# Two layers of windowed attention and FFT convolution on one core: products one block ahead of the PV sums with two logit buffers, kernel rows permuted inside layer A, and the kernel's spectrum stored once and loaded to both halves

## The chip, the cores and the metric

The kernel runs on one core of a Trainium2 chip. The core has five engines that run their own instruction streams and wait for each other on semaphores: PE (TensorE, matrix products), DVE (VectorE), ACT (ScalarE), POOL (GpSimd) and SP (SyncE, which here only issues DMAs). The metric is the device time of one execution in microseconds, as the median of several.

## The reference

Four residual layers on one sequence of 2048 positions with 512 channels: attention, convolution, attention, convolution, each on a layer norm of x.

```python
x = A_x
x = x + _A_ref(_layernorm(x, axis=-1), A_wqkv, A_wo)
x = x + _B_ref(_layernorm(x, axis=-1), B_A_re, B_A_im, ..., B_log_dt, B_Dskip)
x = x + _A_ref(_layernorm(x, axis=-1), A_wqkv, A_wo)
x = x + _B_ref(_layernorm(x, axis=-1), B_A_re, B_A_im, ..., B_log_dt, B_Dskip)
```

Layer A has 32 heads of 16 channels. A position attends to eight positions only: itself and those 2, 4, ... 14 before it.

```python
off = jnp.arange(W) * dil                     # W, dil = 8, 2
idx = pos[:, None] - off[None, :]
...
logits = jnp.einsum("bhsd,bhswd->bhsw", q, kg) * scale
logits = jnp.where(mask[None, None, :, :], logits, -1e9)
attn = _softmax(logits, axis=-1)
o = jnp.einsum("bhsw,bhswd->bhsd", attn, vg)
return (...)(o, 0, 2, 1, 3).reshape(B, S, D) @ wo
```

Layer B convolves each channel with a kernel of 2048 taps, through a Fourier transform of length 4096. The taps come from 128 complex exponentials per channel and are the same in both B layers.

```python
K = jnp.einsum("dn,dnl,dn->dl", Cc, P, dB).real
...
Kf = rfft2(K padded to 2L);  Uf = rfft2(u padded to 2L)
y = irfft2(Uf * Kf)[..., :L] + u * Dskip
```

## The kernel before, in words

The program has these stages, one behind the other: the taps K are made and written to DRAM (`kd_dram`), together with the constants of the transforms and the front of attention layer A0; core A0; layer B0; the front of A1, mixed with the end of B0; core A1; layer B1. The times of the stages stand in the table of the next section.

**Placement of work.** Code is written in Python in the order in which a tile scheduler places it; each engine then runs its own instructions in a fixed order and waits on semaphores. Tiles come from pools with a number of buffers; an instruction that writes a tile of a full pool waits until the last user of that buffer is done. So the order of the calls and the sizes of the pools set what an engine meets next. All DMAs named below are issued by SP, in one row.

**Front of A** (`front_block`): norm of four row tiles (`xn`, applied by `ln_apply` on ACT or DVE by a list of engines), transposition by PE into `xnT`, and the projection of k into `kT_ext`.

**Core of A** (`core`): the 2048 positions are 16 tiles of 128, in four blocks q of four tiles. What a block needs:
- `qproj(q)`: 16 products on PE (L201) into four tiles `pq`, which ACT copies to `qT` (L203).
- `linit(q)`: PE writes the mask into the logit tile L (pool `ps_l`).
- `prod(q, i)`, i = 0 to 7: one DVE product of q with four shifted k (`prod`, L223, 128x2048), then 16 products on PE that sum over the channels of a head into L (L226).
- `sm_a(q)`: DVE takes the maximum (mx, L233), PE subtracts it, ACT takes the exponential (ex, L238). `sm_b(q)`: DVE sums in three steps (s, s, ssum, L244 to L248), inverts (rs, L251), and multiplies (attn, L253). The two together are the softmax chain.
- `pav(q, al)` for each tile al: two DVE products of attn with shifted v (`pav`, L264, 128x2048), which PE sums into `po` (L268); ACT copies it to `o_sb` (L271).
- `out_proj(q, al)`: PE transposes into `pt`, ACT copies to `oT` (L281), PE multiplies with `wop` into `pw` (L284; the profile calls the tile pq), and DVE adds it to the residual x_sb (L72). `pt`, `pw`, the pq of qproj and those of v share the pool `ps_q`.
- `norm_u`: the norm for layer B that follows, written into `xnT`.

`v_proj(a)` makes a tile of v on PE from `wvp` (L299), ACT copies it into `v_ext` (L301), and behind each fourth tile SP issues DMAs that copy v shifted by a position (L305, L306).

The calls are in this order before: block 0's products with all 16 v_proj between them, qproj(1); then, for each block, its softmax chain with the first four products of the next block inside, and its pav with the last four products of the next block and the qproj of the one after between them. [...]

**Taps for B0.** The taps are loaded from `kd_dram` in the row order that the transform wants by 18 DMAs (`k_load`, tile `k_rl`), called ahead of core A0. Behind the core `Dskip` is added to the first row and four copies, on DVE and ACT by turns, permute it into `k_perm` (L881).

**Layer B** (`FftB`): `f1` is the first stage of the transform (L510, 8 chunks per half of the channels; result `a1s`), `f2` the second (L519, with the 4 MB table `w_sb`, 8 chunks). In B0 they run on the taps too: `k_f2` casts a chunk to `kf_sb`, and two DMAs store it, each 64 partitions (the real or the imaginary part), twice, into two copies in `kf_dram` (L528). `u_f2` loads a chunk of 128 partitions (`kf_c`, L540, three buffers), ACT copies the input's spectrum to `ub`, and DVE makes two products t (L543, L544). `i1` and `i2` transform back; i2 reads the tables G2r and G2i. The evacuations of PSUM by `evac` (L499) go to ACT and DVE by turns.

Of the kernel before, what the change touches and what calls it, by code (L numbers as in the profile page):

```python
# [11 lines left out]
ALU = mybir.AluOpType  # L12
# [6 lines left out]
P = 128  # L19
# [87 lines left out]
class LayerA:  # L107
# [66 lines left out]
    def core(self, x_sb, u):  # L174
# [5 lines left out]
        with ExitStack() as c2:  # L180
# [7 lines left out]
            ps_q = c2.enter_context(tc.tile_pool(name=f"a{l}_ps_q", bufs=4, space=PSUM))  # L188
            ps_l = c2.enter_context(tc.tile_pool(name=f"a{l}_ps_l", bufs=1, space=PSUM))
# [170 lines left out]
def build_b_consts(nc, cpool, tmp, w2_dram):  # L360
# [78 lines left out]
    C["G2r"] = cpool.tile([P, 16, P], BF16, name="G2r"); C["G2i"] = cpool.tile([P, 16, P], BF16, name="G2i")  # L439
    for h in range(4):  # L440
        tb = tmp.tile([P, 4, P], I32, name="g2_base")
        nc.gpsimd.iota(tb[:], pattern=[[1, 4], [16, P]], base=4 * h, channel_multiplier=0)
        for nm, bias in (("G2r", 2048.0), ("G2i", 4096.0)):
# [4 lines left out]
            nc.scalar.activation(C[nm][:, h * 4:(h + 1) * 4, :], gi[:], ACT.Sin, bias=s8 * 4096, scale=-s8)  # L448
# [17 lines left out]
class FftB:  # L466


    def __init__(self, tc, nc, C, w2_dram, kf_dram, lnst, x_sb, tag):
        self.tc, self.nc, self.C, self.kf_dram, self.lnst, self.x_sb = tc, nc, C, kf_dram, lnst, x_sb  # L470
        self.w2_dram = w2_dram
        self.tag = tag
        self.c_grp, self.c_mid, self.c_ps = ExitStack(), ExitStack(), ExitStack()
        self.grp = self.c_grp.enter_context(tc.tile_pool(name=f"b{tag}_grp", bufs=5))
        self.ps = self.c_ps.enter_context(tc.tile_pool(name=f"b{tag}_ps", bufs=4, space=PSUM))
        self.nev = 0
        self.S = [dict() for _ in range(NG)]

    def open_mid(self):
        tc, nc, t = self.tc, self.nc, self.tag  # L480
        w2p = self.c_mid.enter_context(tc.tile_pool(name=f"b{t}_w2", bufs=1))
# [3 lines left out]
        self.kfp = self.c_mid.enter_context(tc.tile_pool(name=f"b{t}_kf", bufs=3))  # L485
        self.wk = self.c_mid.enter_context(tc.tile_pool(name=f"b{t}_wk", bufs=3))
# [7 lines left out]
    def evac(self, dst, src, eng=None):  # L494
        nc = self.nc
        if eng is None:
            eng = "act" if self.nev % 2 == 0 else "dve"
            self.nev += 1
# [24 lines left out]
    def k_f2(self, g):  # L523
        def consume(p2, ec):
            kf = self.wk.tile([P, DQG, EC], BF16, name="kf_sb")
            self.evac(kf[:], p2[:].rearrange("p e q -> p q e"))
            for ri in range(2):
                self.nc.sync.dma_start(self.kf_dram[g, ec, :, :, ri].rearrange("u p q e -> p u q e"),  # L528
                                       kf[ri * 64:(ri + 1) * 64].unsqueeze(1).to_broadcast([64, 2, DQG, EC]))
        yield from self.f2(g, "ka", consume)  # L530

    def u_f2(self, g):
        nc = self.nc
        t1 = self.gtile("t1", [P, DQG, P])
# [29 lines left out]
    def i2(self, g, rows_done, xo=None):  # L564
# [3 lines left out]
        for t in range(NA // 4):  # L568
            p4 = self.ptile([P, 4, DQG * 4])
            for j in range(4):  # L570
                a = t * 4 + j
                nc.tensor.matmul(p4[:, j, :], lhsT=C["G2r"][:, a, :], rhs=z[:, a, :], start=True, stop=False)
                nc.tensor.matmul(p4[:, j, :], lhsT=C["G2i"][:, a, :], rhs=z[:, NA + a, :], start=False, stop=True)
# [194 lines left out]
def k_load(tc, nc, kr, kd):  # L768
# [179 lines left out]
```

## Time and profile before

| | us |
|---|---|
| median of 3 runs | 637.56 (636.64 to 638.2) |
| the profiled execution | 638.53 |
| its span (first to last instruction) | 636.8 |
| taps, constants, front of A0 | 0 to about 150 |
| core A0 | to about 298 |
| layer B0 | to about 404 |
| front of A1 | to about 441 |
| core A1 | to about 571 |
| layer B1 | to the end |

Busy in the profiled execution: PE 390.3 us (61% of the span), DVE 479.0 (75%), ACT 355.2 (56%), POOL 42.8 (7%). The granted TensorE clock is 0.83 on average.

A group in the profile is named by its line, its engine and the tiles it writes and reads (`prod<-qT,kT_ext`). "x2" means two such instructions; [6.23 <-ACT qT L203] means that the engine was idle for 6.23 us before it, until ACT had written qT. In a table of waits the columns are the engine and the line of what waited, what it waited for, and then us in total, how often, and the longest. A table of stretches gives for each window its length, the busy time of each engine with its number of instructions, the granted clock, the share of DMA time and GB/s.

### The profile page before, as it was taken

Reading aid. Unit: us, or ns where it says so; the run is one execution under the profiler, and the core shown is the slowest. Engines: PE = TensorE matmul, PEld = TensorE weight load, DVE = VectorE, ACT = ScalarE, POOL = GpSimd, SP = SyncE. Lnnn points to the kernel's source line nnn. Section 1 sums busy time; section 2 is a strip of 40 time slices with the busy share of each in tenths; the row PEclk is TensorE's granted clock in tenths of the full one; section 3 lists DMA queues with packets and bytes.
Section 4 is the critical chain, followed back from the end, with each engine's and each line's share of the span. In section 5 each row is a group of like instructions: output and inputs, shape, how many; then the busy total and the mean of one; then the engine's idle time right before and its main releaser. Section 6 shows DMA issues by size and latency. Waiting matters only on the chain.

```text
span 636.8 us, 11210 instructions
## 1 busy us (share of the span) xinstructions
PE 390.3 (61%) x4536; PEld 251.3 (39%) x4536; DVE 479.0 (75%) x825; ACT 355.2 (56%) x605; POOL 42.8 (7%) x47
## 2 busy tenths in 40 slices
PE   1002234365862995865767377399978867558675
PEld 1001032244431453423657277244444333228664
DVE  3889999985464999884555678856688979848776
ACT  3999888976640354346645362496514243348631
POOL 1001021013100001010000000410000010100000
PEclk9999767876975898888977688799969777798779
DMA  6001210201398000000977872200300000253823
GB/s 189 1 0 59 106 68 33 86 3 39 58 316 188 1 2 1 2 0 2 362 216 205 284 257 71 68 0 17 100 2 1 1 1 3 97 223 125 265 87 132
DMA packets 30070, 58.37 MB, mean 92 GB/s; under 512 B 11193, under 2 KB 17210, under 8 KB 28466
## 3 DMA queue, kind: packets, MB, share of 16 engines
q1 hardware_dynamic: 27138, 50.84, 25.9%
q0 software_dynamic: 576, 4.19, 2.1%
q10 hardware_dynamic: 2304, 2.62, 1.3%
q8 instruction: 35, 0.57, 0.4%
q14 instruction: 17, 0.14, 0.1%
HBM read 36.57 MB, written 15.34 MB: 82 GB/s over the span
## 4 chain that ended last, share of the span: by engine, by line
DVE 34%; PE 31%; ACT 14%; DMA 10%; issue 5%; POOL 3%; SPq 1%; DVEq 0%; POOLq 0%; ACTq 0%
PE po L268 8%; DMA kf_c<-kf_dram 5%; DVE prod L223 4%; PE pq L299 4%; PE pb L510 3%; DVE x_sb L72 3%; PE pq L284 3%; DVE pav L264 3%; POOL ln_rstd L94 3%; PE pq L201 2%; DVE t L543 2%; ACT ln_junk L76 2%; DVE t L544 2%; DVE cm_a L612 2%; DVE cm_b L613 1%
## 5 line engine op out<-in xcount | busy, mean ns | idle before, releaser
L223 DVE TENSOR_TENSOR prod<-qT,kT_ext 128x2048 bf16<-128x2048 bf16 x64 | 76.1, 1217 | 20.4 <-ACT qT L203 17.8
L268 PE MATMUL po<-pav,ident 128*128 128x512 bf16 x256 | 76.8, 441 | 21.2 <-DVE pav L264 21.1
L264 DVE TENSOR_TENSOR pav<-attn,v_ext 128x2048 bf16<-128x2048 bf16 x64 | 75.3, 1219 | 7.0 <-DMA v_ext<-v_ext 5.6
L271 ACT CAST o_sb<-po 128x512 bf16<-128x512 f32 x32 | 18.7, 584 | 74.2 <-PE po L268 74.2
L268 PEld LDWEIGHTS <-ident 128*128 128x128 bf16 x256 | 27.2, 109 | 59.0 <-issue 42.2
L558 PE MATMUL pb<-Wp,t 128*128 128x128 bf16 x256 | 38.7, 245 | 17.8 <-DVE t L543 16.4
L519 PE MATMUL pb<-a1s,w_sb 128*128 128x64 bf16 x768 | 35.0, 206 | 20.0 <-ACT ub L542 6.7
L226 PE MATMUL L<-ind,prod 128*128 128x8 bf16 x1024 | 33.6, 167 | 22.2 <-DVE prod L223 22.2
L148 PE MATMUL pt<-ident,xn 128*128 128x128 bf16 x128 | 13.2, 256 | 51.7 <-DVE xn L104 49.6
L94 POOL TENSOR_TENSOR ln_rstd<-ln_veps,ln_mh 128x4 f32<-128x4 f32 x16 | 21.1, 1320 | 340.5 <-DVE ln_veps L92 317.9
L499 ACT CAST a1s<-pb 128x1024 bf16<-128x1024 f32 x30 | 30.1, 1016 | 24.4 <-PE pb L510 24.0
L542 ACT CAST ub<-pb 128x1024 bf16<-128x1024 f32 x32 | 32.3, 1023 | 19.3 <-DVE t L544 17.8
L226 PEld LDWEIGHTS <-prod 128*128 128x128 bf16 x1024 | 30.9, 99 | 29.6 <-DVE prod L223 24.6
L76 ACT ACTIVATE ln_junk<-x_sb 128x512 bf16<-128x512 f32 x48 | 30.3, 632 | 18.5 <-DVE x_sb L72 16.5
L519 PEld LDWEIGHTS <-w_sb 128*128 128x128 bf16 x768 | 31.2, 106 | 23.5 <-issue 18.1
L284 PE MATMUL pq<-wop,oT 128*128 128x512 bf16 x128 | 34.0, 389 | 10.5 <-ACT oT L281 10.1
L559 PE MATMUL pb<-WpJ,t 128*128 128x128 bf16 x256 | 38.0, 246 | 0.4 <-DVE t L544 0.3
L154 PE MATMUL pp<-xnT,wqk 128*128 128x512 bf16 x128 | 32.9, 398 | 7.4 <-ACT xnT L150 4.2
L746 PE MATMUL pk<-B_r,A_r 128*128 128x84 bf16 x128 | 18.5, 267 | 28.9 <-DVE A_r L614 28.9
L558 PEld LDWEIGHTS <-t 128*128 128x128 bf16 x256 | 28.2, 111 | 17.1 <-DVE t L543 17.0
L72 DVE SCALAR_TENSOR_TENSOR x_sb<-pq,x_sb 128x512 f32<-128x512 f32 x32 | 22.0, 687 | 15.9 <-PE pq L284 15.9
L543 DVE TENSOR_TENSOR t<-ub,kf_c 128x1024 bf16<-128x1024 bf16 x32 | 22.1, 690 | 14.4 <-DMA kf_c<-kf_dram 11.9
(205 smaller groups left out, 1017.7 us busy)
## 6 DMA issues: line engine op xcount, KB each, us to landing
kf_c<-kf_dram SPq DMA_DIRECT2D x32, 512.0 KB, 4.7
w_sb<-w_dram SPq DMA_DIRECT2D x8, 1024.0 KB, 11.2
kf_dram<-kf_sb SPq DMA_DIRECT2D x32, 256.0 KB, 3.8
x_sb<-in_A_x_dram POOLq DMA_DIRECT2D x4, 1024.0 KB, 10.0
v_ext<-v_ext SPq DMA_DIRECT2D x6, 448.0 KB, 6.1
wqk<-in_A_wqkv_dram SPq DMA_DIRECT2D x4, 512.0 KB, 4.8
xin<-in_A_x_dram SPq DMA_DIRECT2D x4, 512.0 KB, 9.2
w_dram<-w_full SPq DMA_DIRECT2D x4, 512.0 KB, 2.6
```

The lines of the kernel that those rows point to most:

```text
L72: nc.vector.scalar_tensor_tensor(x_row, y_psum, 1.0, x_in, ALU.mult, ALU.add, accum_out=lnst["s1"][:, a, part:part + 1])
L76: nc.scalar.activation(lnst["junk"][:], x_row, ACT.Square, accum_out=lnst["s2"][:, a:a + 1])
L94: nc.gpsimd.tensor_tensor(rstd[:], veps[:], lnst["mh"][:, 0:n], ALU.pow)
L223: nc.vector.tensor_tensor(pr[:], qT[:, ft].unsqueeze(1).to_broadcast([P, NW, 4, P]), kap, ALU.mult)
L226: nc.tensor.matmul(L[:, al, w0 + wi, ft * 8:(ft + 1) * 8], lhsT=pr[:, wi, al, :], rhs=ind8[:], start=False, stop=True, skip_group_check=True)
L264: nc.vector.tensor_tensor(pv[:], attn[:, al, wg * NW:(wg + 1) * NW, :].unsqueeze(2).to_broadcast([P, NW, DH, H]), vap, ALU.mult)
L268: nc.tensor.matmul(po[:], lhsT=ident[:], rhs=pv[:, wi].rearrange("p d h -> p (d h)"), start=(w == 0), stop=(w == W - 1))
L284: nc.tensor.matmul(pw[:], lhsT=oT[:, ftp, :], rhs=wo[:, ftp, :], start=(ftp == 0), stop=(ftp == NDT - 1))
L519: nc.tensor.matmul(p2[:, j, :], lhsT=self.w2[:, ec * EC + j, :], rhs=a1s[:, ec * EC + j, :], start=True, stop=True)
L543: nc.vector.tensor_tensor(t1[:, :, ec * EC:(ec + 1) * EC], ub[:], kc[:, 0], ALU.mult)
L558: nc.tensor.matmul(p3[:, j, :], lhsT=t1[:, dql, :], rhs=wp_r, start=True, stop=False)
L559: nc.tensor.matmul(p3[:, j, :], lhsT=t2[:, dql, :], rhs=wpj_r, start=False, stop=True)
```

## The change

**1. Core.** Products run one more block ahead: those of blocks 0 and 1 ahead of the first pav, then two of block q+2 behind each tile's pav of block q; blocks 2 and 3 have pav alone. The softmax chain of block q+1 is split around the pav of block q. The projections of v move from block 0's products to block 1's. Two blocks' logits are alive at once, so `ps_l` has two buffers; `ps_q` has two instead of four.

```diff
-            ps_q = c2.enter_context(tc.tile_pool(name=f"a{l}_ps_q", bufs=4, space=PSUM))
-            ps_l = c2.enter_context(tc.tile_pool(name=f"a{l}_ps_l", bufs=1, space=PSUM))
+            ps_q = c2.enter_context(tc.tile_pool(name=f"a{l}_ps_q", bufs=2, space=PSUM))
+            ps_l = c2.enter_context(tc.tile_pool(name=f"a{l}_ps_l", bufs=2, space=PSUM))
...
                 prod(0, i)
-                if i % 2 == 1:
-                    for a in range(2 * (i - 1), 2 * (i + 1)):
-                        v_proj(a)
-            qproj(1)
+                if i == 3:
+                    qproj(1)
+                    linit(1)
+            sm_a(0)
+            for i in range(8):
+                v_proj(2 * i)
+                v_proj(2 * i + 1)
+                prod(1, i)
+                if i == 3:
+                    sm_b(0)
             for q in range(4):
                 n1 = q + 1 if q + 1 < 4 else None
                 n2 = q + 2 if q + 2 < 4 else None
-                sm_a(q)
                 if n1 is not None:
-                    linit(n1)
-                    prod(n1, 0)
-                    prod(n1, 1)
-                sm_b(q)
-                if n1 is not None:
-                    prod(n1, 2)
-                    prod(n1, 3)
+                    sm_a(n1)
+                if n2 is not None:
+                    qproj(n2)
+                    linit(n2)
                 for al in range(4):
                     pav(q, al)
+                    if al == 1 and n1 is not None:
+                        sm_b(n1)
                     if al > 0:
                         out_proj(q, al - 1)
-                    if al == 1 and n2 is not None:
-                        qproj(n2)
-                    if n1 is not None:
-                        prod(n1, 4 + al)
+                    if n2 is not None:
+                        prod(n2, 2 * al)
+                        prod(n2, 2 * al + 1)
                 out_proj(q, 3)
                 for qq in ((), (0, 1), (2,), (3,))[q]:
                     norm_u(qq)
+                if hook is not None:
+                    hook(q)
```

DVE in core A0, before, from the normaliser of block 0 (attn_1899) to the first pav; L_1852 and attn_2203 are of block 1:

```order
L253 TENSOR_TENSOR attn_1899<-ex_1847,rs_1897 128x1024
L223 TENSOR_TENSOR prod_2024<-qT_1821,kT_ext_101 128x2048
L223 TENSOR_TENSOR prod_2071<-qT_1821,kT_ext_101 128x2048
L223 TENSOR_TENSOR prod_2118<-qT_1821,kT_ext_101 128x2048
L233 TENSOR_REDUCE mx_2150<-L_1852 128x128
L244 TENSOR_TENSOR s4_2195<-ex_2151 128x512
L246 TENSOR_TENSOR s2_2197<-s4_2195 128x256
L248 TENSOR_TENSOR ssum_2199<-s2_2197 128x128
L251 RECIPROCAL rs_2201<-ssum_2199 128x128
L253 TENSOR_TENSOR attn_2203<-ex_2151,rs_2201 128x1024
L264 TENSOR_TENSOR pav_1938<-attn_1899,v_ext_1516 128x2048
```

The same place in the changed kernel; attn_1885 is of block 0, L_1672 and attn_2119 of block 1, qT_2017 of block 2:

```order
L253 TENSOR_TENSOR attn_1885<-ex_1748,rs_1883 128x1024
L233 TENSOR_REDUCE mx_2011<-L_1672 128x128
L223 TENSOR_TENSOR prod_2060<-qT_2017,kT_ext_102 128x2048
L244 TENSOR_TENSOR s4_2111<-ex_2012 128x512
L246 TENSOR_TENSOR s2_2113<-s4_2111 128x256
L223 TENSOR_TENSOR prod_2078<-qT_2017,kT_ext_102 128x2048
L248 TENSOR_TENSOR ssum_2115<-s2_2113 128x128
L223 TENSOR_TENSOR prod_2135<-qT_2017,kT_ext_102 128x2048
L251 RECIPROCAL rs_2117<-ssum_2115 128x128
L223 TENSOR_TENSOR prod_2153<-qT_2017,kT_ext_102 128x2048
L253 TENSOR_TENSOR attn_2119<-ex_2012,rs_2117 128x1024
L264 TENSOR_TENSOR pav_2046<-attn_1885,v_ext_1518 128x2048
```

Block 1's chain stands ahead of the first pav in both. Now four products of block 2 stand between its steps. In all, 16 products precede the first pav in core A0 before, and 20 now; in core A1, 14 and 19.

**2. Taps.** `k_load` and the permutation run inside core A0, in two halves of 256 channels, behind blocks 1 and 2, through one half-sized buffer. All four copies are on ACT.

```diff
+    def k_half(h):
+        hs = slice(h * 256, (h + 1) * 256)
+        kr = krp.tile([P, NA, D // 2], BF16, name="k_rl")
+        k_load(tc, nc, kr, kd, hs)
+        nc.vector.tensor_tensor(kr[0:1, 0, :], kr[0:1, 0, :], dsk[:, hs], ALU.add)
+        for h2 in range(2):
+            nc.scalar.copy(kp[:, h * 64 + h2 * 32:h * 64 + (h2 + 1) * 32, :, :],
+                           kr[:, :, h2 * 128:(h2 + 1) * 128].rearrange("p a (q r) -> p q a r", r=4))
+
+    la.core(x_sb, u, lambda q: k_half(q - 1) if q in (1, 2) else None)
```

SP in core A0, before, where v_ext is shifted:

```order
L787 DMA k_rl<-kd_dram 32x2x512
L787 DMA k_rl<-kd_dram 64x5x512
L787 DMA k_rl<-kd_dram 64x7x512
L787 DMA k_rl<-kd_dram 64x4x512
L172 DMA wop<-in_A_wo_dram 32x4x512 x4
L305 DMA v_ext<-v_ext 112x1024
L306 DMA v_ext<-v_ext 15x1024
```

And in the changed kernel:

```order
L780 DMA kd_dram<-kgs 1x64
L172 DMA wop<-in_A_wo_dram 32x4x512 x4
L305 DMA v_ext<-v_ext 112x1024
L306 DMA v_ext<-v_ext 15x1024
L305 DMA v_ext<-v_ext 112x2048
L306 DMA v_ext<-v_ext 15x2048
L305 DMA v_ext<-v_ext 112x2048
L306 DMA v_ext<-v_ext 15x2048
L787 DMA k_rl<-kd_dram 16x16x256
```

The loads of k_rl stood ahead of all shifts of v_ext; now they follow, but for one between the last two pairs.

**3. Spectrum.** `kf_dram` holds the spectrum once. A chunk is stored by two DMAs of half the size as before and loaded by two DMAs of 64 partitions each, one to either half of a slot of `kf_ring`, which has four slots.

```diff
-                self.nc.sync.dma_start(self.kf_dram[g, ec, :, :, ri].rearrange("u p q e -> p u q e"),
-                                       kf[ri * 64:(ri + 1) * 64].unsqueeze(1).to_broadcast([64, 2, DQG, EC]))
+                self.nc.sync.dma_start(self.kf_dram[g, ec, :, ri], kf[ri * 64:(ri + 1) * 64])
...
-            kc = self.kfp.tile([P, 2, DQG, EC], BF16, name="kf_c")
-            nc.sync.dma_start(kc[:], self.kf_dram[g, ec].rearrange("u p i q e -> (u p) i q e"))
+            kc = self.kf_ring[:, self.nkf % 4]
+            self.nkf += 1
+            for h in range(2):
+                nc.sync.dma_start(self.kf_ring[h * 64:(h + 1) * 64, (self.nkf - 1) % 4], self.kf_dram[g, ec])
```

SP from the end of core A0 through layer B0, before:

```order
L306 DMA v_ext<-v_ext 15x2048
L878 DMA dskip<-in_B_Dskip_dram 1x512
L484 DMA w_sb<-w_dram 128x4096 x4
L528 DMA kf_dram<-kf_sb 64x2x1024 x32
L540 DMA kf_c<-kf_dram 128x2048 x16
```

And in the changed kernel:

```order
L803 DMA k_rl<-kd_dram 64x4x256
L493 DMA w_sb<-w_dram 128x4096 x4
L494 DMA g_sb<-g_dram 128x4096
L541 DMA kf_dram<-kf_sb 64x1024 x32
L556 DMA kf_ring<-kf_dram 64x2048 x32
```

The stores keep their number at half the elements, the loads double in number at half the size, and all loads of B0 still follow all its stores.

**4. Smaller parts.** The tables G2r and G2i are no longer resident: while the constants are made, they are written to `g2_dram` by eight DMAs, through one buffer `g2_s`, and each layer B loads them (`g2_sb`, 1 MB, L494). In the front of A1 three of four norm applications go to DVE instead of two: `["act", "dve", "act", "dve"]` became `["act", "dve", "dve", "dve"]`. Four pools of layer B got the option by which a buffer's waits are kept for each tile apart (`reuse_waits="tile"`).

More of the change, by code (lines that the diff above doesn't have):

```diff
@@ L496, in evac @@
         if eng is None:
-            eng = "act" if self.nev % 2 == 0 else "dve"
+            eng = self.pat[self.nev % len(self.pat)]
             self.nev += 1
@@ L866 @@
     krctx = ExitStack()
-    krp = krctx.enter_context(tc.tile_pool(name="kr", bufs=1, side="right"))
-    kr = krp.tile([P, NA, D], BF16, name="k_rl")
-    k_load(tc, nc, kr, kd)
-    la.core(x_sb, u)
-    z0 = xnT[:].rearrange("p t c -> p (t c)").rearrange("p (m c) -> p m c", m=2 * NA)
-    fb = FftB(tc, nc, C, w2_dram, kf_dram, lnst, x_sb, 0)
-    fb.z0 = z0
-    kp = fb.gtile("k_perm", [P, P, NA, 4])
-    with tc.tile_pool(name="dsk", bufs=1) as dp:
-        dsk = dp.tile([1, D], BF16, name="dskip")
-        nc.sync.dma_start(dsk[:], ins["Dskip"].partition_broadcast(1))
-        nc.vector.tensor_tensor(kr[0:1, 0, :], kr[0:1, 0, :], dsk[:], ALU.add)
-    for h in range(4):
-        (nc.vector.tensor_copy if h % 2 == 0 else nc.scalar.copy)(
-            kp[:, h * 32:(h + 1) * 32, :, :], kr[:, :, h * 128:(h + 1) * 128].rearrange("p a (q r) -> p q a r", r=4))
-    krctx.close()
-    la.close()
+    kpp = krctx.enter_context(tc.tile_pool(name="kp", bufs=1))
+    kp = kpp.tile([P, P, NA, 4], BF16, name="k_perm", tag="kp")
+    krctx2 = ExitStack()
+    krp = krctx2.enter_context(tc.tile_pool(name="kr", bufs=1, side="right"))
+    dsk = krp.tile([1, D], BF16, name="dskip")
+    nc.sync.dma_start(dsk[:], ins["Dskip"].partition_broadcast(1))
+    def k_half(h):
[7 more added lines that the diff above has]
+    la.core(x_sb, u, lambda q: k_half(q - 1) if q in (1, 2) else None)
+    krctx2.close()
+    la.close()
+    z0 = xnT[:].rearrange("p t c -> p (t c)").rearrange("p (m c) -> p m c", m=2 * NA)
+    fb = FftB(tc, nc, C, w2_dram, g2_dram, kf_dram, lnst, x_sb, 0)
+    fb.z0, fb.ring_pool = z0, kpp
     fb.open_mid()
```

54 lines of the change are left out of this document (33 added, 21 removed).

## The prediction

> **What bounds the kernel now.** I read the table of stretches first, cut at the stages, to see which engine fills which stage (columns: window, length, busy time of PE, PEld, DVE, ACT, POOL, granted TensorE clock, DMA share, GB/s).
>
> ```profile
> 178.00:206.00 28.00, 11.49 (x154) 6.17 (x152) 15.66 (x20) 6.27 (x9) 0.00 (x0) 0.61 1.10 246
> 206.00:260.00 54.00, 44.15 (x414) 22.42 (x414) 51.34 (x72) 22.68 (x46) 2.04 (x2) 0.85 0.01 1
> 260.00:298.00 38.00, 24.64 (x137) 10.62 (x135) 27.19 (x50) 17.86 (x37) 2.92 (x2) 0.94 0.00 0
> ...
> 318.00:348.00 30.00, 20.26 (x427) 18.37 (x426) 16.05 (x14) 14.04 (x15) 0.00 (x0) 0.73 0.73 211
> 348.00:386.00 38.00, 20.62 (x379) 18.94 (x375) 26.75 (x38) 18.30 (x19) 0.36 (x1) 0.77 0.72 239
> 404.00:441.00 37.00, 27.94 (x164) 13.80 (x162) 22.80 (x58) 28.32 (x52) 10.04 (x5) 0.86 0.13 30
> ...
> 467.00:520.00 53.00, 44.05 (x344) 21.10 (x344) 44.72 (x60) 20.91 (x41) 1.01 (x1) 0.80 0.00 1
> 520.00:571.00 51.00, 33.21 (x260) 15.42 (x258) 39.48 (x70) 19.47 (x42) 3.92 (x3) 0.82 0.22 84
> ```
>
> Both attention cores are DVE's: 51.34 of 54 us, then 27.19 of 38 in the first; 44.72 of 53 and 39.48 of 51 in the second. The exception is 178 to 206, where DVE works 15.66 of 28 us while DMA is full. From 318 to 348, storing the kernel's spectrum, no engine is full (PE 20.26 of 30) and DMA is 0.73 busy.
>
> Next I read what DVE waited for, by stage: the first core, the first layer B, the second core (columns: us in total, times, longest).
>
> ```profile
> DVE prod L223 <- ACT qT L203: 14.3, 4, 6.2
> DVE x_sb L72 <- PE pq L284: 6.0, 5, 1.8
> DVE pav L264 <- DMA v_ext<-v_ext: 5.6, 1, 5.6
> DVE mx L233 <- PE L L226: 4.8, 3, 3.4
> DVE s L244 <- ACT ex L238: 4.7, 3, 2.2
> ```
>
> ```profile
> DVE kf_sb L499 <- DMA kf_dram<-kf_sb: 11.0, 7, 5.4
> DVE a1s L499 <- PE pb L510: 10.0, 8, 2.8
> DVE t L543 <- DMA kf_c<-kf_dram: 8.9, 9, 3.2
> ```
>
> ```profile
> DVE x_sb L72 <- PE pq L284: 9.9, 9, 1.8
> ...
> DVE s L244 <- ACT ex L238: 3.2, 3, 1.3
> DVE mx L233 <- PE L L226: 3.1, 3, 1.3
> ```
>
> So there are three targets: the head of core A0, where pav waits for the shifted copies of v; the softmax chain (mx, Exp on ACT, s), met when DVE has nothing else ready; and the spectrum stores, on which 11.0 us of kf_sb casts wait.
>
> **Term 1, head of core A0.** The timeline of SP, then of DVE:
>
> ```profile
> 184.50 4.94 SPq L787 DMA_DIRECT2D k_rl<-kd_dram  x5
> ...
> 192.64 0.59 SPq L305 DMA_DIRECT2D v_ext<-v_ext  x1
> ```
>
> ```profile
> 156.43 2.36 DVE L223 TENSOR_TENSOR prod<-qT,kT_ext 128x2048 bf16<-128x2048 bf16 x2 [6.23 <-ACT qT L203]
> 162.34 1.23 DVE L223 TENSOR_TENSOR prod<-qT,kT_ext 128x2048 bf16<-128x2048 bf16 x1 [3.54 <-ACT qT L203]
> ```
>
> ```profile
> 205.90 1.22 DVE L264 TENSOR_TENSOR pav<-attn,v_ext 128x2048 bf16<-128x2048 bf16 x1 [5.59 <-DMA v_ext<-v_ext]
> ```
>
> SP issues the last loads of k_rl from 184.50 on, and only at 192.64 the first v_ext shift; the first pav starts at 205.90. The change takes k_rl out of that place, so the shifts follow the projections of v, and DVE's own work sets the first pav. A prod costs 2.36/2 = 1.18 us. What one softmax chain costs DVE, and where it stands, the second core's head shows:
>
> ```profile
> 453.09 1.23 DVE L233 TENSOR_REDUCE mx<-L 128x128 bf16<-128x1024 f32 x1 [1.33 <-PE L L226]
> 457.83 3.50 DVE L223 TENSOR_TENSOR prod<-qT,kT_ext 128x2048 bf16<-128x2048 bf16 x3 [3.52 <-ACT qT L203]
> 461.35 0.43 DVE L244 TENSOR_TENSOR s<-ex 128x512 bf16<-128x512 bf16 x1
> ...
> 462.48 1.23 DVE L223 TENSOR_TENSOR prod<-qT,kT_ext 128x2048 bf16<-128x2048 bf16 x1
> 463.62 0.95 DVE L251 RECIPROCAL rs<-ssum 128x128 bf16<-128x128 f32 x1
> ...
> 465.56 0.68 DVE L253 TENSOR_TENSOR attn<-ex,rs 128x1024 bf16<-128x1024 bf16 x1
> ...
> 467.29 1.22 DVE L264 TENSOR_TENSOR pav<-attn,v_ext 128x2048 bf16<-128x2048 bf16 x1
> ```
>
> The three sums run from 461.35 to the prod at 462.48, 1.13 us; with mx, rs and attn a chain is 1.23 + 1.13 + 0.95 + 0.68 = 3.99 us. In DVE's order of before, 16 prods and two chains precede the first pav; now it is 20 prods and two chains. Two prods run before 162.34, so 18 x 1.18 + 2 x 3.99 = 29.2 us follow. I add the longest wait of each kind that the stage shows, 3.4 (mx) and 2.2 (ex), and get 162.3 + 29.2 + 5.6 = 197: 8.9 us earlier, with four more prods done (4 x 1.18 = 4.7 us). Gain 13.6 us. Ends: no more than the v_ext wait of 5.6 us, where something else holds the copies; or 19 us, where the waits vanish too.
>
> **Term 2, rest of core A0.** Chains a block ahead spare what is left of the mx and ex waits: 4.8 + 4.7 less the 5.6 already used is 3.9 us; I take half, 2. Against it stands ps_q with two buffers instead of four: the pt and pw tiles of one output projection fill both, and the next waits for DVE's residual add (x_sb, L72). Ends 4 better to 6 worse, the latter the whole x_sb wait over again. The k_perm copies go to ACT in this stage: 2 x 3.70 us by the row below, on an ACT that is busy 22.68 of 54 and 17.86 of 38 us. An o_sb or oT behind such a pair is late by up to 3.7 us, twice; I cost it at nothing, since in block 1 DVE has two prods to do between the pavs of one tile and the next; for block 2, where no prods are left as cover, up to 4 us stand in the ends.
>
> **Term 3, core A0 to layer B.**
>
> ```profile
> 293.43 0.69 DVE L72 SCALAR_TENSOR_TENSOR x_sb<-pq,x_sb 128x512 f32<-128x512 f32 x1 [0.97 <-PE pq L284]
> ...
> 298.07 1.29 DVE L881 COPY k_perm<-k_rl 128x2048 bf16<-128x2048 bf16 x2 [0.55 <-ACT xnT L102]
> ```
>
> ```profile
> 298.07 3.70 ACT L881 COPY k_perm<-k_rl 128x2048 bf16<-128x2048 bf16 x2
> ```
>
> ```profile
> 298.97 5.16 PE pb L510 x96
> ```
>
> The first transform (f1, L510) now starts at 298.97, after the last norm and the first k_perm copy. With k_perm built inside the core, only PSUM must be free, which the last residual add gives: 293.43 + 0.69 = 294.1. Gain 4.8 us; the ends are 0 (its casts queue behind the norm on DVE and ACT) and 5. The w_sb loads, which wait for k_perm now, come earlier by more than f1 does, so they aren't late next; g2_sb adds one transfer behind them, used much later.
>
> **Term 4, spectrum stores.**
>
> ```profile
> 308.80 39.85 SPq L528 DMA_DIRECT2D kf_dram<-kf_sb  x32
> ```
>
> ```profile
> 320.17 1.08 PE pb L510 x16
> ...
> 324.72 1.01 PE pb L519 x16
> ```
>
> Sixteen chunks take 39.85 us, 2.49 each. Halving the bytes takes the DMA from 0.73 busy to about 0.37, and then PE is next: one group of L510 and one of L519, 1.08 + 1.01 = 2.09 us, x16 = 33.4. Gain 6.4 us. Ends: 9 with a higher granted clock than 0.73, and 3 where the casts' other wait (a1s for PE, 10.0 us) grows.
>
> **Term 5, spectrum loads.** Each chunk's load becomes two of 64 partitions, in a ring of four instead of three. Chunks run from 354.46 to 384.47:
>
> ```profile
> 354.46 0.69 DVE L543 TENSOR_TENSOR t<-ub,kf_c 128x1024 bf16<-128x1024 bf16 x1 [3.16 <-DMA kf_c<-kf_dram]
> ```
>
> ```profile
> 384.47 0.68 DVE L544 TENSOR_TENSOR t<-ub,kf_c 128x1024 bf16<-128x1024 bf16 x1
> ```
>
> That is 30.7/16 = 1.92 us each. The fourth slot can take back part of the 8.9 us of load waits; the first load still goes out behind the last store, so the 3.16 us of first fill stay. I put 0, with ends of 6 better and, by the next row, 18 worse over both layers. The nearest row for 64-partition transfers is the store stretch, 211 GB/s; at that rate a chunk's 524 KB take 2.48 us, 0.56 more than now, x32 = 18 us. I stay at 0 because there half the time nothing was to be sent (0.73 busy): 211/0.73 = 289 GB/s while busy makes 1.81 us a chunk, under the 1.92.
>
> [...]
>
> **Term 6, front and core of A1.** Four norm applications go from ACT to DVE, which has room there (22.80 of 37 us against ACT's 28.32): I put 1 us, ends 0 and 3, the latter if ACT bounds the whole stage.
>
> In the core five more prods and one mx stand ahead of the first pav: 5 x 1.18 + 1.23 = 7.1 us moved into the head, whose 3.52 us of qT wait can cover part; I put the first pav at 469.5, 2.2 later than 467.29, so 5 us gained. Of the mx and ex waits, 3.1 + 3.2, I take 3. Gain 8, ends 2 and 14. Layer B1 has no stores; 0.
>
> The eight stores of the G2 table before core A0 and the DMAs for it replace two resident tiles; ACT's next Sin waits for the previous store. I put 0, 1 either way.
>
> **Sum.** 13.6 + 2 + 4.8 + 6.4 + 0 + 1 + 8 = 35.8 us. The terms are from one execution of 638.53 us (span 636.8), 0.97 above the median of 637.56; against the median: 637.56 - 35.8 = 601.8.
>
> **Rivals.** A: forecast, 592 to 612. B: the cores stay as slow per block as now, DVE waiting elsewhere (x_sb for pq grew from 6.0 to 9.9 between the cores); then terms 2 and 6 give 0 or -4 and the gain is 13.6 + 4.8 + 6.4 - 4 = 21: 617. For it: DVE already works 51.34 of 54 us from 206 to 260, so nothing is to be had there; against it: 44.72 of 53 and 39.48 of 51 in the second core. C: half loads at the row's 211 GB/s, term 5 at -18: 620. D, the other side: two pq buffers. Each of 32 output projections waits for the residual add of the one before, which stands on DVE behind up to two prods and a pav (2 x 1.18 + 1.22 = 3.6 us). The change is undone from 35.8/32 = 1.12 us per projection on the path; at 1.5 us it takes 650. Against it: the waits of L72 today go the other way, DVE for PE. E: all waits in the cores gone, k_f2 at 1.9 us a chunk: 36 + 5 + 6 + 3 = 50, 588.
>
> **Chances.** A 0.55, B 0.17, C 0.12, D 0.05, E 0.08; 0.03 for a failure that leaves the time unchanged. The range 586 to 622 takes in A, B, most of E and C. A difference within 0.3% (2 us) can't be told from none. Faster 0.92, same 0.03, slower 0.05.
>
> **What would show it.** First pav near 197, f1 less than 1 us after the last residual add; sixteen stores' chunks in about 33 us with no kf_sb wait for DMA; u_f2 chunks at or under 1.92 us (2.5 is C); mx and s waits of DVE near zero in both cores. D would show as PE waiting for DVE x_sb ahead of L284 or the transposes. Wrong outright if the first pav waits for v_ext still, or ACT's k_perm pairs leave PE waiting for oT.

## The result, and the profile after

The changed kernel takes 603.33 us (601.58 to 605.19) against 637.1 for the kernel before on the same chip: a ratio of 0.9472, 95% interval 0.9437 to 0.9507. The forecast was 601.8, the range 586 to 622. The profiled execution has a span of 599.8 us, 37.0 less than before. The sum was right, and three of its terms were wrong by 6 to 10 us, not all in one direction. That the time came out so near is in part luck, as the account below shows. (In `e1_core_only` and `e10_prefetch` one execution of four was disturbed and slower; their times below are the medians of the other three, and in `e1_core_only` it was the profiled one, so that no durations are read from its trace.) The table of the stages shows them; every time in it is the start (or, for a "last", the end) of the row named, in the timelines of the two profiled executions.

| from row to row | before | after | gained | forecast |
|---|---|---|---|---|
| start to first pav of A0 | 205.9 | 196.7 | 9.2 | 8.9 |
| to the end of A0's last residual add | 88.2 | 79.5 | 8.7 | 6.7 |
| to the first f1 matmul | 4.9 | 0.1 | 4.8 | 4.8 |
| to the first spectrum store | 9.8 | 10.6 | -0.8 | 0 |
| to the end of the last store's issue | 39.9 | 26.9 | 13.0 | 6.4 |
| to the first product t | 5.8 | 6.4 | -0.6 | 0 |
| to the last product t of B0 | 30.7 | 36.3 | -5.6 | 0 |
| to the first ln_rstd of A1 | 19.2 | 20.6 | -1.4 | 0 |
| to the first pav of A1 | 62.9 | 66.3 | -3.4 | -1.2 |
| to the end of A1's last residual add | 100.9 | 82.8 | 18.1 | 10.1 |
| to the last product t of B1 | 44.3 | 48.7 | -4.4 | 0 |
| to the end of the span | 24.3 | 24.9 | -0.5 | 0 |

The forecast's 4.7 us for the four products stand in the second row with term 2's 2; term 6 is spread over the rows to and behind A1's first pav (front 1, first pav 2.2 later, 7.1 us of work moved ahead and 3 of waits).

The table of stretches of the changed kernel, in the columns explained above, cut at its own stages:

```profile
197.00:241.00 44.00, 36.12 (x335) 18.65 (x342) 42.80 (x58) 20.00 (x37) 0.00 (x0) 0.92 0.08 20
...
287.00:314.00 27.00, 19.85 (x549) 17.57 (x550) 18.77 (x17) 17.45 (x18) 0.00 (x0) 1.00 0.68 151
...
320.00:338.00 18.00, 5.09 (x76) 4.44 (x76) 10.35 (x16) 7.47 (x8) 0.00 (x0) 0.51 1.04 229
...
443.00:491.00 48.00, 39.18 (x377) 20.12 (x383) 47.12 (x63) 18.39 (x37) 0.00 (x0) 0.93 0.06 16
```

DVE is now busy 42.80 of 44 us behind the first pav of A0 and 47.12 of 48 in A1: hardly a wait is left in these two stretches. In the store stretch (287 to 314) TensorE is granted its full clock, where it had 0.73 on average. From 320 to 338, the loads of the spectrum, DMA is full (1.04) at only 229 GB/s, and DVE works 10.35 of 18 us.

What DVE waited for in core A0 from the first pav on, and from A1's front through core A1:

```profile
DVE x_sb L72 <- PE pq L284: 5.3, 4, 3.0
DVE pav L264 <- DMA k_rl<-kd_dram: 2.5, 1, 2.5
```

```profile
DVE ln_nb L96 <- POOL ln_rstd L94: 6.8, 7, 1.2
DVE kT_ext L157 <- PE pp L154: 6.7, 6, 2.1
DVE x_sb L72 <- PE pq L284: 5.0, 3, 2.6
DVE mx L233 <- PE L L226: 2.1, 2, 1.7
```

No wait of s for ex is left among the longer ones, mx waits 2.1 instead of 3.1 us, and x_sb's waits for pq fell from 9.9 (nine times) to 5.0 (three times). Ahead of the first pav of A0 the gain in such waits is smaller: from 150 on, mx still waits 4.7 us there (4.8 in all of core A0 before), s 0.2 (4.7), and prod for qT 8.9 (14.3). And the first pav itself still waits for DMAs:

```profile
196.72 1.23 DVE L264 TENSOR_TENSOR pav<-attn,v_ext 128x2048 bf16<-128x2048 bf16 x1 [2.49 <-DMA k_rl<-kd_dram]
```

In layer B0 the list reads:

```profile
DVE t L559 <- DMA kf_ring<-kf_dram: 10.5, 9, 2.6
DVE kf_sb L512 <- DMA kf_dram<-kf_sb: 5.1, 4, 1.7
DVE a1s L512 <- PE pb L523: 3.7, 5, 1.2
```

The kf_sb casts still wait 5.1 us for stores (11.0 before), and the products t wait longer than before for their loads (10.5 against 8.9 us). The DMA issues, from the page (KB each, median us to landing):

```profile
kf_ring<-kf_dram SPq DMA_DIRECT2D x64, 256.0 KB, 7.2
...
kf_dram<-kf_sb SPq DMA_DIRECT2D x32, 128.0 KB, 3.4
```

A load of half the size lands after 7.2 us, where 512 KB took 4.7.

### The profile page after: what moved, and what is told of

It reads as the page before. It is cut to its first block, busy times and chain, and to the rows that moved or that the text cites. A ratio compares the mean times of both kernels' runs of the same rounds, so it can differ in the third digit from the quotient of the medians.

```text
span 599.8 us, 11233 instructions
## 1 busy us (share of the span) xinstructions
PE 373.9 (62%) x4496; PEld 242.2 (40%) x4536; DVE 475.8 (79%) x828; ACT 356.8 (59%) x603; POOL 44.8 (7%) x47
## 4 chain that ended last, share of the span: by engine, by line
DVE 34%; PE 26%; DMA 12%; ACT 11%; issue 9%; SPq 3%; POOL 3%; DVEq 0%; POOLq 0%; ACTq 0%; another core or an unknown queue 0%
DMA kf_ring<-kf_dram 5%; DVE pav L264 5%; PE po L268 4%; PE pq L299 4%; DVE prod L223 3%; POOL ln_rstd L94 3%; PE pq L201 3%; PE pb L523 2%; DMA v_ext<-v_ext 2%; PE pq L284 2%; DVE cm_a L628 2%; PE L L226 2%; PE pp L154 2%; DMA kf_dram<-kf_sb 2%; DVE x_sb L72 2%
## 5 line engine op out<-in xcount | busy, mean ns | idle before, releaser
L268 PE MATMUL po<-pav,ident 128*128 128x512 bf16 x245 | 69.2, 402 | 19.7 <-DVE pav L264 18.0
L268 PEld LDWEIGHTS <-ident 128*128 128x128 bf16 x256 | 25.8, 103 | 51.1 <-issue 30.6
L76 ACT ACTIVATE ln_junk<-x_sb 128x512 bf16<-128x512 f32 x48 | 30.2, 630 | 26.9 <-DVE x_sb L72 26.7
L94 POOL TENSOR_TENSOR ln_rstd<-ln_veps,ln_mh 128x4 f32<-128x4 f32 x16 | 23.1, 1444 | 307.8 <-DVE ln_nm L87 154.7
L226 PEld LDWEIGHTS <-prod 128*128 128x128 bf16 x1024 | 32.8, 96 | 21.8 <-DVE prod L223 12.2
L532 PE MATMUL pb<-a1s,w_sb 128*128 128x64 bf16 x768 | 32.3, 199 | 12.3 <-ACT ub L558 8.2
L226 PE MATMUL L<-ind,prod 128*128 128x8 bf16 x1024 | 35.0, 167 | 6.4 <-DVE prod L223 6.2
L574 PEld LDWEIGHTS <-t 128*128 128x128 bf16 x256 | 28.4, 112 | 24.3 <-DVE t L559 24.2
L762 PE MATMUL pk<-B_r,A_r 128*128 128x84 bf16 x128 | 18.1, 263 | 30.8 <-DVE A_r L630 30.7
L532 PEld LDWEIGHTS <-w_sb 128*128 128x128 bf16 x768 | 28.4, 102 | 15.3 <-issue 11.6
L559 DVE TENSOR_TENSOR t<-ub,kf_ring 128x1024 bf16<-128x1024 bf16 x32 | 22.0, 686 | 14.6 <-DMA kf_ring<-kf_dram 14.6
L201 PE MATMUL pq<-xnT,wqk 128*128 128x512 bf16 x121 | 31.9, 386 | 2.5 <-ACT qT L203 1.3
## 6 DMA issues: line engine op xcount, KB each, us to landing
x_sb<-in_A_x_dram POOLq DMA_DIRECT2D x4, 1024.0 KB, 10.6
```

The lines of the kernel that those rows point to most:

```text
L94: nc.gpsimd.tensor_tensor(rstd[:], veps[:], lnst["mh"][:, 0:n], ALU.pow)
L201: nc.tensor.matmul(pq[:], lhsT=wqk[:, dt, ft * P:(ft + 1) * P], rhs=xnT[:, dt, q * 512:(q + 1) * 512], start=(dt == 0), stop=(dt == NDT - 1))
L226: nc.tensor.matmul(L[:, al, w0 + wi, ft * 8:(ft + 1) * 8], lhsT=pr[:, wi, al, :], rhs=ind8[:], start=False, stop=True, skip_group_check=True)
L268: nc.tensor.matmul(po[:], lhsT=ident[:], rhs=pv[:, wi].rearrange("p d h -> p (d h)"), start=(w == 0), stop=(w == W - 1))
L532: nc.tensor.matmul(p2[:, j, :], lhsT=self.w2[:, ec * EC + j, :], rhs=a1s[:, ec * EC + j, :], start=True, stop=True)
L574: nc.tensor.matmul(p3[:, j, :], lhsT=t1[:, dql, :], rhs=wp_r, start=True, stop=False)
```

## The experiments

The ratios are against the kernel before on the same chip. The first four kernels part the change.

**Core alone (`e1_core_only`).** The kernel before with the new `core` of part 1, word for word, and nothing else.

> The kernel before with the new order of the core and its PSUM split (two pq, two L), and nothing else: the 18 loads of k_rl stay ahead of core A0, the spectrum is stored twice. Theory (the head of core A0 needs both the order and the freed queue): the shifts of v_ext still go out at about 192 to 200, so the first pav stays near 205.9; what comes behind it shortens as in the changed kernel (8.7 us), core A1 gives its 14.7 us (18.1 behind its first pav less 3.4 ahead of it), the front of A1 nothing: 637 - 23 = 614 us. Rival (the order alone makes the head): 9.2 us more, 604 to 605.

Measured: 607.6 us, ratio 0.9532 (0.9482 to 0.9583), between the two. SP's rows and the first pav:

```profile
170.14 17.24 SPq L792 DMA_DIRECT2D k_rl<-kd_dram  x17
188.53 2.58 SPq L172 DMA_DIRECT2D wop<-in_A_wo_dram  x4
191.21 0.59 SPq L305 DMA_DIRECT2D v_ext<-v_ext  x1
```

```profile
208.16 1.16 DVE L264 TENSOR_TENSOR pav<-attn,v_ext 128x2048 bf16<-128x2048 bf16 x1
```

All loads of k_rl still go out ahead of the first v_ext shift, and the first pav comes at 208, not at 197: the order alone doesn't make the head. But DVE doesn't wait for v_ext there, as it did before for 5.59 us. The scheduler has placed the same calls in another order: 24 products and three chains, the last without its attn, stand ahead of that pav, where the changed kernel has 20 products and two chains. At the prediction's prices these are 4 x 1.18 + 3.31 = 8.0 us of work that is done early and is missing behind the pav, so the late pav costs less than the theory's 9.2 us. The order alone brings some 30 us (a ratio of 0.9532 on 638.1), the whole change 33.8.

**Core undone (`e4_old_core`).** The changed kernel with the `core` of before and a call of the hook added to it.

> The changed kernel with part 1 undone: the core in the order of before, with four pq and one L buffer; taps in the core, spectrum stored once, G2 loaded. Theory: core A1 goes back by 14.7 us, core A0 behind the first pav by 8.7; the head keeps part of its gain, since the shifts of v_ext need not wait for k_rl, at most the 5.6 us that pav waited before: 603 + 23 + 4 = 630 us. Rival (the k_rl loads alone held the head): first pav near 197 to 198, 626 to 627 us.

Measured: 637.2 us, ratio 0.9976 (0.9952 to 1.0001). Both expectations were too low: without the new order the rest of the change brings nothing. In its trace the head did move, and the time was given back. The first row is its first pav; the next two are what DVE waited for from there to the end of the core, with its table of stretches:

```profile
193.82 1.23 DVE L264 TENSOR_TENSOR pav<-attn,v_ext 128x2048 bf16<-128x2048 bf16 x1 [4.16 <-DMA k_rl<-kd_dram]
```

```profile
DVE x_sb L72 <- PE pq L284: 13.2, 11, 2.9
DVE pav L264 <- DMA k_rl<-kd_dram: 4.2, 1, 4.2
```

```profile
206.00:260.00 54.00, 40.89 (x377) 20.79 (x380) 44.59 (x69) 26.38 (x42) 3.87 (x2) 0.75 0.08 20
```

First pav 12.1 us earlier than before, but 103.4 us from there to the last residual add instead of 88.2. DVE waits 13.2 us for output projections, where it waited 6.0, and works 44.59 of the 54 us from 206 to 260 instead of 51.34; the granted clock there is 0.75 instead of 0.85. Before, the softmax chain of block 1 was done ahead of the wait for v_ext; here it comes behind the first pav, with one of the products. A head that starts sooner with less work done ahead is not a gain. Of the 13.2 us, the three longest waits (7.4 us) stand in the last block, from 287 on, where no copy of k_perm runs any more (the last starts at 243.94); so the copies don't explain the most of it. What the lower clock takes isn't parted from the rest by any run. Part of why nothing is left lies elsewhere: this kernel also has part 3, which loses time as it stands (below).

**Spectrum stored twice again (`e2_stored_twice`).** Part 3 undone, the ring of four slots kept:

```diff
-                self.nc.sync.dma_start(self.kf_dram[g, ec, :, ri], kf[ri * 64:(ri + 1) * 64])
+                self.nc.sync.dma_start(self.kf_dram[g, ec, :, :, ri].rearrange("u p q e -> p u q e"),
+                                       kf[ri * 64:(ri + 1) * 64].unsqueeze(1).to_broadcast([64, 2, DQG, EC]))
...
-            for h in range(2):
-                nc.sync.dma_start(self.kf_ring[h * 64:(h + 1) * 64, (self.nkf - 1) % 4], self.kf_dram[g, ec])
+            nc.sync.dma_start(kc, self.kf_dram[g, ec].rearrange("u p i q e -> (u p) i q e"))
```

> The changed kernel with part 3 undone but for the four slots: the spectrum is stored twice and a chunk is loaded by one DMA of 128 partitions. Theory (storing once gives 13 us, loading by halves of 64 partitions takes 10 us): B0's store stretch goes back from 26.9 to about 39 us, the chunks of u_f2 go from 2.27 to 1.9 us or less in both layers; sum +2 to +4, about 606 us. Rival (the loads are slow because of the ring or the waits, not the 64 partitions): loads stay at 2.2 us a chunk, about 616 us.

Measured: 590.2 us, ratio 0.9263 (0.923 to 0.9295): 13 us faster than the changed kernel, where both theories had it slower. SP's rows, and the stretch of the loads:

```profile
287.44 37.32 SPq L541 DMA_DIRECT2D kf_dram<-kf_sb  x32
324.86 25.62 SPq L556 DMA_DIRECT2D kf_ring<-kf_dram  x16
```

```profile
331.00:345.00 14.00, 6.73 (x96) 6.09 (x96) 11.48 (x18) 8.36 (x9) 0.00 (x0) 0.50 0.94 325
```

The stores go back by 10.4 us, as expected. But the products t of a layer now take 25.6 us in B0 (36.3 in the changed kernel) and 25.1 in B1 (34.6), a pace of 1.6 us a chunk: better than before (30.7 and 30.3), so the four slots may have a gain of their own that the half loads hid. The next kernel tests it.

**Three slots (`e7_ring3`).** That kernel with `[P, 3, 2, DQG, EC]` and `% 3`.

> The kernel e2_stored_twice with three slots in the ring instead of four, one DMA of 128 partitions for each chunk. Theory (before, the loads were bound by latency over three buffers, so that the fourth slot gives what the two layers gain, 1.92 to 1.6 us a chunk): 590 + 10 = 600 us, 1.9 us a chunk. Rival (the fourth slot is not what counts, but the finer waits of the pools): 590 us.

Measured: 599.9 us, ratio 0.9374 (0.9319 to 0.9429). The stretches of t are 30.5 and 31.3 us, as before the change. The fourth slot alone is worth some 10 us over both layers (61.8 us of these stretches against 50.7). But for the finer waits of the ring, this kernel is the change without its part 3: against `e1_core_only` (0.9532), parts 2 and 4 bring it to 0.9374, and part 3 takes the changed kernel back to 0.9472. In the same window DMA is no longer full:

```profile
331.00:345.00 14.00, 4.61 (x71) 4.01 (x70) 9.64 (x16) 7.08 (x7) 0.00 (x0) 0.50 0.73 240
```

With three slots the loads wait for room (0.73 busy, 240 GB/s), with four they fill the DMA (0.94, 325 GB/s).

**Halves from two copies (`e9_halves_two_copies`).** `e2_stored_twice` with its load split into halves, each from its own copy, to part two causes.

```diff
-            nc.sync.dma_start(kc, self.kf_dram[g, ec].rearrange("u p i q e -> (u p) i q e"))
+            for h in range(2):
+                nc.sync.dma_start(self.kf_ring[h * 64:(h + 1) * 64, (self.nkf - 1) % 4], self.kf_dram[g, ec, h])
```

> The kernel e2_stored_twice (590.2 us) with one edit: a chunk is loaded by two DMAs of 64 partitions, each from its own stored copy. It tells two causes of the slow loads apart, both halves reading one place in DRAM, or the 64 partitions. Theory (64 partitions): the chunks of u_f2 go to 2.2 to 2.3 us in both layers, DMA full at about 229 GB/s, 590 + 20 = 610 us. Rival (reading one place twice): 1.6 us a chunk as in e2, 590 us.

Measured: 611.3 us, ratio 0.9567 (0.9513 to 0.9622).

```profile
331.00:345.00 14.00, 4.05 (x64) 3.56 (x63) 7.77 (x12) 5.75 (x6) 0.00 (x0) 0.50 1.04 246
```

The same bytes from the same places, cut at partition 64: 246 GB/s at a DMA share of 1.04, against 325 at 0.94, and 21 us more. So it is the cut at partition 64, not the place that is read. A load is also half as large, and no run cuts it in half another way. But its packets are as large as those of the whole load (some 4 KB in both windows), and DMA is full, so the packets themselves take longer: by share and rate, 4 KB cost 1.04 x 16 x 4096 B / 246 GB/s = 0.28 us of an engine's time, against 0.94 x 16 x 4096 B / 325 GB/s = 0.19 us in the window of `e2_stored_twice`. It isn't the gaps between loads. Why the packets take longer, no run shows.

**Two queues (`e5_two_queues`).** The changed kernel with the upper halves issued by ACT (`for h, q in enumerate((nc.sync, nc.scalar)): q.dma_start(...)`).

> The changed kernel with one edit: of the two loads of a chunk, the lower half of the partitions stays on SP's queue and the upper half is issued by ACT, so that both halves are under way at once. [...] Rival (the sum of the halves is limited whatever the queue): 2.27 us a chunk, 603 us, or more by ACT's issues.

Measured: 593.8 us, ratio 0.9288 (0.9249 to 0.9328): 9.5 us faster than the changed kernel, but not by faster transfers.

```profile
320.00:335.00 15.00, 5.46 (x92) 4.71 (x88) 9.32 (x15) 6.07 (x6) 0.00 (x0) 0.62 0.99 225
```

```profile
q1 hardware_dynamic: 597, 1.92, 56.7%
q10 hardware_dynamic: 431, 1.44, 41.6%
```

Both queues are at work in that window (packets, MB, share), and together they move 225 GB/s at a share of 0.99: no more than one queue. The time came from elsewhere: with ACT's halves off SP's row, loads no longer stand behind all stores, and the first t starts at 315.96, 0.9 us ahead of the last store's issue end instead of 6.4 behind it. That is 4.2 us, of which B0's products t, in 38.3 instead of 36.3 us, give 2.0 back. The rest of the 9.6 us between the two spans is spread over the later stages, 3.3 of it behind the last t of B1, and stays unexplained.

**One load for both halves (`e3_one_load`).** The changed kernel with a single DMA that reads the chunk twice, by a leading dimension of step zero: `nc.sync.dma_start(kc, bass.AP(tensor=src.tensor, offset=src.offset, ap=[[0, 2]] + [list(x) for x in src.ap]))`.

> The changed kernel with one edit: a chunk is stored once and loaded by one DMA that reads it twice into all 128 partitions, instead of two DMAs of 64. [...] Rival (reading one place twice, or the ring, is the limit): no change, 603.

Measured: 817.6 us, ratio 1.2821 (1.2794 to 1.2847). It was expected to be faster or, by the rival, the same; both were wrong. The DMA view from 327 to 470:

```profile
DMA packets 1855, 7.51 MB, mean 53 GB/s; under 512 B 28, under 2 KB 28, under 8 KB 1852
...
q1 hardware_dynamic: 1852, 7.47, 12.8%
```

A share of 12.8% is about that of two of the sixteen engines (2/16 = 12.5%), at 53 GB/s where the half loads had 229. Why this load runs so, no run shows.

**Three pq (`e8_pq3`).** `ps_q` with three buffers, `ps_o` with one.

> The changed kernel with three pq buffers instead of two and one po instead of two. Theory (two pq buffers cost nothing, since DVE waits for the output projection only in the tails): no gain, 603; one po buffer may cost up to 0.6 us a tile, up to 620. Rival D of the prediction (projections wait for a pq slot): less than 600.

Measured: 609.5 us, ratio 0.9546 (0.9495 to 0.9598), 6 us slower than the changed kernel. Both cores are longer (86.7 and 85.8 us from the first pav to the last residual add, instead of 79.5 and 82.8; some 2.8 us of A0's difference is a product, an rs and an attn that stand ahead of the pav in the changed kernel and behind it here). In core A0 PE now waits for the copy of po, which it doesn't in the changed kernel:

```profile
PE po L268 <- ACT o_sb L271: 9.4, 6, 3.4
```

So the second po is worth more than a third pq; since this run changes both, pq alone isn't measured. Against rival D speaks the trace of the changed kernel: its list of PE's waits from either first pav to the last residual add has none for x_sb.

**The old split of the norm (`e11_old_split`).** `["act", "dve", "act", "dve"]` in the changed kernel.

> The changed kernel with one edit: the norm applications of A1's front go to ACT and DVE by turns again. Term 6 of the prediction gave the new split 1 us. Theory now (DVE stands still for 5.9 us beside the memset, so that a third application on DVE waits behind it): the stretch from the first ln_rstd of A1 to the first pav gets 1 to 2.5 us shorter, 601 to 603 us. Rival (the new split helps): 604 to 606.

Measured: 601.9 us, ratio 0.9412 (0.9361 to 0.9463). The stretch to A1's first pav is 64.0 us instead of 66.3, as the theory said, but that is no gain: 17 products stand ahead of that pav now, where the changed kernel has 19, and these two, at 1.18 us each, make the 2.3 us. From that pav to the last residual add it takes 85.8 instead of 82.8 us, so front and core together take 149.8 instead of 149.1, and the time as a whole can't be told from 603.3. Neither split is shown to be better.

**GpSimd's memset (`e6_zero_dma`, `e12_before_zero_dma`).** In the front of A1, in every kernel so far, one POOL row lies beside a row of DVE. The timelines of POOL and of DVE in the changed kernel:

```profile
378.06 6.06 POOL L308 MEMSET v_ext<- 1x7168 bf16 x1
```

```profile
378.23 5.92 DVE L85 TENSOR_SCALAR ln_nm<-ln_nm 128x4 f32<-128x4 f32 x1
```

A tensor_scalar of 128x4 that takes 0.16 us elsewhere takes 5.92, until the memset ends. By what the one holds up the other, the trace doesn't show. Both experiments replace `nc.gpsimd.memset(v[0:1, 0:14, :], 0.0)` by a DMA from a row of zeros in DRAM.

> The kernel e2_stored_twice (590.2 us) with one edit: the first row of v_ext is cleared by a DMA of zeros instead of GpSimd's memset. In the front of A1 that memset runs 6.06 us, and DVE's tensor_scalar at its side takes 5.9 us, before and after the change alike. Theory (DVE stands still because of the memset): the front shortens by 4 to 6 us, about 585 us. Rival (the front is bound by something else then): within 1 us of 590.

> The kernel before with one edit: the first row of v_ext is cleared by a DMA of zeros instead of GpSimd's memset, in both layers. Theory (DVE's tensor_scalar in the front of A1 stands still for as long as the memset runs, and the front waits for it): the stretch from the first ln_rstd of A1 to the first pav falls from 62.9 to 58 or 59 us, 633 us. Rival (in the old order the front is bound by ACT, so that DVE's stop is hidden): within 2 us of 637.6.

Measured on `e2_stored_twice`: 584.6 us, ratio 0.9137 (0.9077 to 0.9197) against 0.9263 (0.923 to 0.9295); the stretch to A1's first pav is 62.1 us instead of 66.3. On the kernel before: 628.8 us, ratio 0.9866 (0.984 to 0.9892); that stretch is 57.6 instead of 62.9. In both pairs the same number of products stands ahead of that pav (19, and 14), so the stretches can be compared. The theory holds, in both orders; on the kernel before, more is gained than these 5.3 us, most of it in core A1 (97.7 instead of 100.9 us from its first pav to its last residual add), which stays unexplained.

**Early loads (`e10_prefetch`).** `e6_zero_dma` with the first four ring loads of B0 ahead of the stores of the second half.

> The kernel e6_zero_dma (584.6 us) with one edit: the first four loads of layer B0's ring are issued ahead of the stores of the second half of the channels, instead of behind all stores. Theory (the fill of the ring, 5.8 us from the last store's end to the first product t, is exposed): 4 to 6 us off, about 580 us. Rival (they only push the stores back): 584 to 586.

Measured: 580.3 us, ratio 0.9102 (0.9024 to 0.918), not told apart from `e6_zero_dma`. The fill is gone (first t at 325.08, before the stores' end at 329.35), but the stores take 43.4 us instead of 38.6: kf_sb's waits for stores are 15.1 us in its list. Both beat the changed kernel and the one before; the least measured is 580.3 us, 9% under the kernel before.

## Why the prediction was right, and where its terms were not

- **What bounds it** held: both cores were DVE's, and what the new order removed is DVE's waits. It is most of the gain: alone it brings some 30 of the 33.8 us, and the rest of the change without it brings nothing (a ratio of 0.9976).
- **Term 1** (13.6 us): first pav at 197 forecast, 196.72 measured, with 20 products and two chains ahead of it as worked out. But "DVE's own work sets the first pav" is not what the trace shows: the pav waits 2.49 us for DMAs, and a wait for v_ext there was a sign by which the forecast would be wrong outright. In the chain of waits the third pair's shift of v_ext takes 13.15 us, and one load of k_rl, which lies between the last two pairs, ends last:

```profile
181.43 13.15 DMA v_ext<-v_ext
...
194.59 2.13 DMA k_rl<-kd_dram
```

The waits from the third product on sum up to 7.8 us instead of 5.6 (4.72 of them mx), the work is 27.7 instead of 29.2, and it starts 1.1 us sooner; that these cancel is luck. The place of k_rl has a smaller worth than the rows say, since with a late pav more work is placed ahead of it (`e1_core_only`).
- **Term 3** (4.8): f1 starts 0.07 us behind the last residual add, for which PE waits. As worked out.
- **Term 2** (2 us): 8.7 less the 4.7 of the products is 4.0; the end given as better was 4. Two pq buffers showed no cost. Nor did the k_perm pairs on ACT: PE's waits for oT in that core are 4.7 us in all, against 5.3 before.
- **Term 4** (6.4 us): mis-sized, 13.0. The step that failed is the price of a pair of matmul groups, 1.08 + 1.01 us. 0.73 was the mean clock of the stretch; these two rows (at 320.17 and 324.72) lie where it was 0.50, and the same chain of waits of before has rows that cost 0.59 and 0.63 where it was 1.00:

```profile
330.19 0.59 PE pb L510 x16
...
331.87 0.63 PE pb L519 x16
```

```profile
330.00:332.00 2.00, 0.89 (x28) 0.77 (x25) 1.23 (x1) 1.01 (x1) 0.00 (x0) 1.00 0.91 298
320.00:322.00 2.00, 1.06 (x16) 0.87 (x16) 1.34 (x2) 0.73 (x1) 0.00 (x0) 0.50 0.86 230
```

In the changed kernel the clock is 1.00 all through, and the pieces are as short:

```profile
311.02 0.64 PE pb L523 x16
311.65 0.57 PE pb L532 x16
```

Together 1.21 us, so PE wasn't next. A chunk takes 26.9/16 = 1.68 us, and four casts still waited for the DMA, with 64-partition stores. The prediction named the higher clock as an end, with 9 us, 4 too few.
- **Term 5** (0): mis-sized, -10.0 over both layers. The step that failed is to carry the rate while busy, 211/0.73 = 289 GB/s, from the stores of before to the loads. For those stores it stands: from 330 to 332, in the rows above, DMA moved 298 GB/s at a share of 0.91. (That half of the time nothing was to be sent is a misreading: 0.73 busy leaves 0.27.) The half loads fill the DMA at 229, and the changed kernel's own stores, whose rows are written once, move 151 at a share of 0.68, or 222 while busy. Why the stores of before moved more, no run shows. Two halves under way from two queues at once moved no more: 225 GB/s at a share of 0.99 in `e5_two_queues`. Rival C's row (2.48 us a chunk) was nearer to the 2.29 us that 524 KB take at 229 GB/s. So of rival C, given 0.12, the slow half loads came, with 10 of its 18 us; its time did not, because terms 4 and 6 were too small by more than that. Against whole loads with the same four slots (`e2_stored_twice`), the half loads cost 20.2 us over both layers.
- **Term 6**: front and core of A1 gave 18.1 - 3.4 = 14.7 us instead of 9. DVE's busy time (the third figure behind the length) tells where, in the two stretches before and then after:

```profile
404.36:467.29 62.93, 49.79 (x442) 25.77 (x440) 43.55 (x77) 39.47 (x70) 10.04 (x5) 0.89 0.18 47
467.29:568.17 100.88, 77.25 (x602) 36.52 (x602) 82.65 (x122) 39.23 (x79) 3.92 (x3) 0.81 0.08 31
```

```profile
377.11:443.44 66.33, 56.78 (x536) 30.11 (x543) 52.72 (x89) 40.29 (x71) 10.04 (x5) 0.92 0.16 45
443.44:526.26 82.82, 64.84 (x490) 30.91 (x500) 73.77 (x113) 36.77 (x74) 5.71 (x3) 0.92 0.17 47
```

DVE's idle time fell by 15.0 us, from 19.4 + 18.2 to 13.6 + 9.0; that is the whole gain. The mx and s waits fell by 3.9 (6.3 to 2.4), near the 3 taken. The step that failed is that no other wait in the core was priced: x_sb's waits for pq, which fell by 4.9 us, weren't counted at all. The 1 us of the split of the norm isn't shown either way (`e11_old_split`).
- **Rivals.** B (617) and D (650) are out: DVE is busy 42.80 of 44 us behind the first pav. A holds, by a sum whose errors cancelled, which is luck: +6.6 at term 4 and +5.7 at term 6, -10 at term 5.
- The part "spectrum stored once" costs 13 us against whole loads with the same four slots: with it undone and the rest kept the kernel is at 590.2.

## What to carry to other kernels

Where one engine is the bound and its waits are for chains through other engines, start the next block's chain a block earlier and price the gain by all the waits of that engine, not only by those the change names. Count the work that stands ahead of a point in the trace before comparing when two kernels reach it; a stretch can be shorter because work has moved out of it. Storing half the bytes (10.4 us won here) is no gain if the loads are then cut at 64 partitions (some 20 us lost): take the rate from transfers of the same direction and shape. Matmul rows from a stretch of lowered clock overstate PE as the next bound (here 1.08 us at a clock of 0.50, 0.59 at 1.00); look at the clock where the row stands.

## What the runs showed of the hardware that was not expected

- Loads of 64 partitions fill the DMA (shares of 0.99 to 1.04) at 225 to 246 GB/s, on one queue or on two at once; of 128 partitions it moved 325 GB/s at a share of 0.94. Stores of 64 partitions with each row written twice moved 298 GB/s at 0.91 (kernel before).
- The loads of `e3_one_load`, whose source begins with a dimension of two and step zero, ran on two engines' worth of DMA (a share of 12.8%), at 53 GB/s.
- A memset of one partition on GpSimd (6.06 us) held a DVE instruction of 0.16 us for 5.92 us, and without it the kernel before is 1.3% faster.
